# 42 unread matmuls on the whole array, on half its rows and on quarters, behind the last output projection of an attention and SwiGLU kernel

## The chip, the core and the metric

The kernel runs on one core of one Trainium2 chip. The metric is the time of one execution on the device, in microseconds (us); lower is better. The number for a kernel is the median of several runs.

## The reference, cut to what matters

Block-sparse attention (a window, global blocks and sampled blocks, given as a mask) is followed by an RMS norm and a gated feed-forward layer:

```python
scores = scale * q @ k^T                      # 4 batches, 8 heads, 768 positions, 64 per head
scores = where(mask, scores, -1e9)
attn = softmax(scores)
x = (attn @ v), heads side by side            # 3072 tokens x 512
xn = x / sqrt(mean(x*x) + 1e-6) * rms_g
g = xn @ w_gate                               # 512 -> 1536
h = g * sigmoid(g) * (xn @ w_val)
out = h @ w_out                               # 1536 -> 512, float32
```

## The kernel before

The 3072 tokens go through in nine groups: three of 256 tokens for the first batch, and two of 384 for each of the other three. For each group and head the kernel multiplies keys by queries (`scores`, L316: `st` tiles on TensorE at L325, then the exponential on ScalarE at L328), and then the exponentials by the values (`values`, L332: `op` tiles at L336; a 65th column of ones gives the softmax sum). The results are scaled by VectorE and gathered in `stage`; after the last head come the norm, a transpose to `xg`, and the feed-forward layer.

The feed-forward layer of a group is a list of pieces made by `ffn_pieces` (L426): 12 `gate` pieces (`gp`, L436), 12 `val` pieces (`vp`, L447), and `down` pieces for the output projection (`yp`, L464). The pieces of one group are put between the attention steps of the next by a hand-written rate (`fill`, `position`), so that TensorE always has something to do. The engines run the order in which the program is written.

The last group has no successor. Its feed-forward layer is run alone at the end of the program: the two-bank score pool `ps_s` is closed (`st_psum.close()`, L754), and a pool `ps_tail` of four one-bank PSUM tiles takes its place for `gp` (L755). `vp` and `yp` stay in the three banks of `ps_f`. The last three token blocks are projected one after another. The last block is cut into two halves of 256 columns, each 12 matmuls into `yp`, then a ScalarE copy with a factor of 0.5 to `yo` (L470), then a store by SyncE's queue (L471). The last thing that TensorE does is the second of these halves.

At the end of the program, which the profile puts on L783, SyncE waits for each outstanding transfer. Each engine executes a drain, which ends when the engine's own work has ended, and raises a semaphore. GpSimd gathers the five and releases all; this is done twice, and then the program is over.

Several matmuls before have no reader either: `keep_busy` (L167) multiplies `idle`, a tile of zeros of 128 rows, by itself, in the first group. One matmul uses fewer than 88 rows: the transpose `trms` of the norm's gains (L672), with 4 rows and 4 columns of float32; its matmul carries the tile size 32 x 128, all others 128 x 128. An instruction that loads the weights (LDWEIGHTS; the profile lists it as engine PEld) stands ahead of each matmul.

```python
nc.tensor.matmul(out=yp, lhsT=hps[:, f, tt * P:(tt + 1) * P], rhs=wo[:, f, lo:hi],
                 start=(f == 0), stop=(f == NF - 1))
```

Of the kernel before, what the change touches and what calls it, by code (L numbers as in the profile page):

```python
# [9 lines left out]
FP32 = mybir.dt.float32  # L10
# [8 lines left out]
def kernel(  # L19
# [17 lines left out]
    nc = tc.nc  # L37
    P = 128
# [90 lines left out]
    for h in range(2):  # L129
        for which, src in ((0, k), (1, q)):  # L130
            f32 = ld.tile([P, NC * D], FP32, name="first", tag="turned", bufs=4)
            cols = 2 * D if which else NC * D
            nc.sync.dma_start(  # L133
                out=f32[:, 0:cols],
# [29 lines left out]
    idle = const.tile([P, 512], BF16, name="idle")  # L164
# [66 lines left out]
    for r in range(NRND):  # L231
        nc.vector.scalar_tensor_tensor(
            out=bm[0:NB, :], in0=samp[0:NB, :, r], scalar=kc[0:NB, :], in1=bm[0:NB, :],
# [3 lines left out]
    for m, (lo, hi) in enumerate(((0, 6), (6, 11), (11, 16))):  # L237
        nc.vector.tensor_scalar(
            out=qmask.rearrange("p (c i r) -> p c i r", c=NC, r=16)[:, 0:2, :, lo:hi],
# [19 lines left out]
    unread = ps_s.tile([P, 1024], FP32, name="unread0", tag="st")  # L259
# [495 lines left out]
    with tc.tile_pool(name="ps_tail", bufs=4, space=bass.MemoryType.PSUM) as ps_tail:  # L755
        for piece in ffn_pieces(ps_tail, groups[-1], pe["xg"], last=True):
            piece()


# [28 lines left out]
```

## Time and profile before

| | |
|---|---|
| median of 3 runs | 314.55 us (313.8 to 314.91) |
| span of the profiled execution | 312.8 us |
| TensorE matmuls, busy | 302.8 us (97%), 2850 recorded |
| weight loads, busy | 201.1 us (64%) |
| VectorE, ScalarE, GpSimd, busy | 202.7, 205.1, 52.9 us |
| granted TensorE clock | 1.000 |

The span is counted from the first to the last instruction of one execution under the profiler. The median of the runs is 1.75 us above it; that part lies around the span. TensorE is busy nearly all the time, and the chain of work that ended last is 86% TensorE. Only at the very end is there a stretch in which TensorE has nothing to do.

A matmul's row in the profile has a start and a modelled end. Neighbouring matmuls overlap in these rows, so what a matmul costs in a row of equal ones is the distance from one start to the next, and not its listed duration. Merged rows give the first start, the time from there to the last end, and the number of instructions; the last start is the end less the listed duration of one.

### The profile page before, as it was taken

Reading aid. Unit: us, or ns where it says so; the run is one execution under the profiler, and the core shown is the slowest. Engines: PE = TensorE matmul, PEld = TensorE weight load, DVE = VectorE, ACT = ScalarE, POOL = GpSimd, SP = SyncE. Lnnn points to the kernel's source line nnn. Section 1 sums busy time; section 2 is a strip of 40 time slices with the busy share of each in tenths; the row PEclk is TensorE's granted clock in tenths of the full one; section 3 lists DMA queues with packets and bytes.
Section 4 is the critical chain, followed back from the end, with each engine's and each line's share of the span. In section 5 each row is a group of like instructions: output and inputs, shape, how many; then the busy total and the mean of one; then the engine's idle time right before and its main releaser. Section 6 shows DMA issues by size and latency. Waiting matters only on the chain.

```text
span 312.8 us, 7261 instructions
## 1 busy us (share of the span) xinstructions
PE 302.8 (97%) x2850; PEld 201.1 (64%) x2869; DVE 202.7 (65%) x557; ACT 205.1 (66%) x332; POOL 52.9 (17%) x79
## 2 busy tenths in 40 slices
PE   8888999999999999999999999999999999999996
PEld 5666886976787566655666566655666566655653
DVE  6978875775578647682767457683777636674860
ACT  4976775777788586667676766766767567632331
POOL 9935132100220122012010122010000100010000
PEclk9999999999999999999999999999999999999999
DMA  7999999999789469605784277714000130002002
GB/s 166 271 210 208 208 265 142 175 227 136 209 147 162 104 134 158 141 20 146 149 152 101 70 182 127 143 40 119 34 2 0 36 118 2 1 2 101 2 0 102
DMA packets 66730, 36.84 MB, mean 118 GB/s; under 512 B 48308, under 2 KB 62288, under 8 KB 66696
## 3 DMA queue, kind: packets, MB, share of 16 engines
q0 software_dynamic: 16064, 17.90, 31.7%
q1 hardware_dynamic: 50596, 18.47, 27.7%
q8 instruction: 22, 0.36, 0.5%
q14 instruction: 12, 0.10, 0.1%
q10 hardware_dynamic: 36, 0.01, 0.0%
HBM read 28.59 MB, written 6.29 MB: 112 GB/s over the span
## 4 chain that ended last, share of the span: by engine, by line
PE 86%; DMA 7%; ACT 3%; DVE 2%; issue 1%; SPq 1%; ACTq 0%
PE yp L464 19%; PE gp L436 19%; PE vp L447 18%; PE st L325 18%; PE op L336 11%; DMA turned<-qbf 4%; ACT ex L328 2%; DMA QT<-turned 2%; DMA first<-in_q_dram 1%; PE tx L418 0%; DVE QT L293 0%; DVE junk L369 0%; DVE stage L362 0%; PE tqk L288 0%; SPq L133 0%
## 5 line engine op out<-in xcount | busy, mean ns | idle before, releaser
L328 ACT ACTIVATE ex<-st 128x768 bf16<-128x768 f32 x192 | 153.9, 812 | 56.2 <-PE st L325 54.5
L325 PE MATMUL st<-QT,KT 88*128 88x384 bf16 (+1 forms) x432 | 93.5, 308 | 1.9 <-DMA QT<-turned 0.7
L451 DVE SCALAR_TENSOR_TENSOR u<-th,gp 128x384 bf16<-128x384 bf16 (+1 forms) x108 | 54.8, 508 | 40.7 <-ACT th L440 39.0
L436 PE MATMUL gp<-xg,wg 128*128 128x384 bf16 (+1 forms) x432 | 80.7, 307 | 0.0
L447 PE MATMUL vp<-xg,wv 128*128 128x384 bf16 (+1 forms) x432 | 80.2, 307 | 0.4 <-DVE u L451 0.4
L464 PE MATMUL yp<-wo,hps 128*128 128x512 bf16 (+1 forms) x284 | 71.6, 369 | 0.9
L440 ACT ACTIVATE th<-gp 128x384 bf16<-128x384 f32 (+1 forms) x108 | 48.9, 453 | 28.9 <-PE gp L436 28.7
L453 DVE TENSOR_TENSOR hps<-u,vp 128x384 bf16<-128x384 bf16 (+1 forms) x108 | 55.1, 510 | 11.4 <-PE vp L447 0.3
L325 PEld LDWEIGHTS <-KT 88*128 88x128 bf16 x432 | 41.7, 98 | 27.0 <-issue 1.9
L447 PEld LDWEIGHTS <-wv 128*128 128x128 bf16 x432 | 40.6, 97 | 20.9 <-issue 0.6
L436 PEld LDWEIGHTS <-wg 128*128 128x128 bf16 x432 | 40.2, 97 | 20.3
L336 PEld LDWEIGHTS <-ex 128*128 128x128 bf16 x1152 | 46.0, 98 | 11.2 <-DVE stage L362 0.8
L336 PE MATMUL op<-Vp,ex 128*128 128x65 bf16 x1152 | 48.8, 194 | 1.6 <-DVE stage L362 0.5
L464 PEld LDWEIGHTS <-hps 128*128 128x128 bf16 x300 | 27.7, 97 | 22.4
L377 POOL TENSOR_TENSOR rstd<-ssq,mhalf 128x3 f32<-128x3 f32 (+1 forms) x9 | 7.3, 815 | 139.4 <-DVE ssq L369 139.4
L345 DVE RECIPROCAL rz<-op 128x3 f32<-128x3 f32 (+1 forms) x64 | 11.2, 174 | 26.2 <-PE op L336 26.1
L470 ACT ACTIVATE yo<-yp 128x512 f32<-128x512 f32 (+1 forms) x25 | 14.4, 576 | 16.0 <-PE yp L464 16.0
L99 POOL DMA_DIRECT2D vraw<-in_v_dram x16 | 12.0, 753 | 69.4 <-DVE Vp L118 60.4
L346 DVE TENSOR_TENSOR stage<-op,rz 128x192 bf16<-128x192 f32 (+1 forms) x64 | 21.8, 341 | 2.2
L369 DVE CUSTOM_DVE_ANT_0 junk<-stage 128x448 bf16<-128x448 bf16 (+1 forms) x24 | 14.8, 618 | 0.6
L389 DVE SCALAR_TENSOR_TENSOR xs<-stage,rstd,gain 128x512 bf16<-128x512 bf16 x15 | 10.4, 748 | 4.4 <-POOL rstd L377 4.4
L87 POOL DMA_DIRECT2D kbf<-in_k_dram x15 | 11.1, 742 | 7.0 <-DMA wo<-in_moe_w_out_dram 7.0
(73 smaller groups left out, 104.6 us busy)
## 6 DMA issues: line engine op xcount, KB each, us to landing
vraw<-in_v_dram POOLq DMA_DIRECT2D x16, 384.0 KB, 5.1
out_dram<-yo SPq DMA_DIRECT2D x23, 256.0 KB, 2.2
kbf<-in_k_dram POOLq DMA_DIRECT2D x15, 192.0 KB, 5.8
qbf<-in_q_dram POOLq DMA_DIRECT2D x12, 192.0 KB, 6.0
KT<-turned SPq DMA_DIRECT2D x24, 96.0 KB, 4.2
QT<-turned SPq DMA_DIRECT2D x24, 96.0 KB, 2.3
wo<-in_moe_w_out_dram POOLq DMA_DIRECT2D x1, 1536.0 KB, 20.5
wg<-in_moe_w_gate_dram POOLq DMA_DIRECT2D x2, 384.0 KB, 9.8
```

The costliest lines, as they stand in the source:

```text
L325: nc.tensor.matmul(out=at[:, e, 0:tg], lhsT=KT[b % 2][0:KR, h, jt * P:(jt + 1) * P], rhs=QT[b % 2][0:KR, h, c0 * P:c0 * P + tg], start=Tru ...
L328: nc.scalar.activation(out=ex[:, nj * part:nj * (part + 1), :], in_=at[:, 0:nj, 0:tg], func=AF.Exp, scale=SCALE)
L336: nc.tensor.matmul(out=op[:, it, 0:VW], lhsT=ex[:, jt, it * P:(it + 1) * P], rhs=Vp[b % 2][:, h, jt, :], start=(jt == 0), stop=(jt == NC - 1))
L346: nc.vector.tensor_tensor(out=stage[:, 0:n, h * D:(h + 1) * D], in0=op[:, 0:n, 0:D], in1=rz[:, 0:n].unsqueeze(2).to_broadcast([P, n, D]), ...
L369: nc.vector.tensor_tensor_reduce(out=junk[:, 0:hi - lo], in0=part, in1=part, scale=1.0, scalar=(e["ssq"][:, it:it + 1] if lo else DM * 1e- ...
L436: nc.tensor.matmul(out=gp[:, 0:tg], lhsT=wg[:, c, f * P:(f + 1) * P], rhs=xg[:, c, 0:tg], start=(c == 0), stop=(c == KD - 1))
L440: nc.scalar.activation(out=th[:, 0:tg], in_=gp[:, 0:tg], func=AF.Tanh, scale=0.5)
L447: nc.tensor.matmul(out=vp[:, 0:tg], lhsT=wv[:, c, f * P:(f + 1) * P], rhs=xg[:, c, 0:tg], start=(c == 0), stop=(c == KD - 1))
L451: nc.vector.scalar_tensor_tensor(out=u[:, 0:tg], in0=th[:, 0:tg], scalar=1.0, in1=gp[:, 0:tg], op0=ALU.add, op1=ALU.mult)
L453: nc.vector.tensor_tensor(out=hps[:, f, 0:tg], in0=u[:, 0:tg], in1=vp[:, 0:tg], op=ALU.mult)
L464: nc.tensor.matmul(out=yp, lhsT=hps[:, f, tt * P:(tt + 1) * P], rhs=wo[:, f, lo:hi], start=(f == 0), stop=(f == NF - 1))
L470: nc.scalar.mul(out=yo, in_=yp, mul=0.5)
```

## The change

Behind the last piece, four new tiles are taken from `ps_tail`. 42 matmuls on `idle` are written to them, and nothing reads them:

```diff
     with tc.tile_pool(name="ps_tail", bufs=4, space=bass.MemoryType.PSUM) as ps_tail:
         for piece in ffn_pieces(ps_tail, groups[-1], pe["xg"], last=True):
             piece()
+        banks = [ps_tail.tile([P, 512], FP32, name="unread", tag="ff") for _ in range(4)]
+
+        def spare(bank, row, rows, cols):
+            nc.tensor.matmul(
+                out=banks[bank][:, 0:cols], lhsT=idle[row:row + rows, 0:P],
+                rhs=idle[row:row + rows, 0:cols], start=True, stop=True)
+
+        def whole(*at):
+            for bank in at:
+                spare(bank, 0, P, 256)
+
+        def halves(*at):
+            for i, bank in enumerate(at):
+                spare(bank, 64 * (i % 2), 64, 256)
+
+        whole(0, 1)
+        halves(2, 3)
+        whole(0, 1)
+        halves(2, 3, 0, 1)
+        whole(2, 3)
+        halves(0, 1, 2, 3, 0, 1)
+        whole(2, 3)
+        for i in range(4):
+            spare(i, 32 * i, 32, 256)
+        whole(0, 1)
+        for cols in (65, 64):
+            for _ in range(8):
+                spare(2, 0, P, cols)
```

That is 10 matmuls of 128 rows and 256 columns, 12 of 64 rows (by turns rows 0 to 63 and 64 to 127), 4 of 32 rows (one on each quarter), and 16 of 128 rows with 65 or 64 columns. In the built program they stand behind the last `yp` matmul on TensorE, each with its own weight load, and none waits for a semaphore or raises one. The matmuls of 64 rows carry the tile size 64 x 128 at row 0 or 64, those of 32 rows 32 x 128 at rows 0, 32, 64 and 96. The instructions of all other engines are the same as before.

## The prediction

> **What bounds the kernel now.** I read the page's chain of waits first (86% TensorE, so the order of TensorE's work sets the end), then the last five microseconds, because all that is added stands there. The timeline from 308 us on, with start and length of each merged row:
>
> ```profile
> 307.74 2.02 PE L464 MATMUL yp<-wo,hps 128*128 128x256 bf16 x17
> 307.79 2.74 SPq L471 DMA_DIRECT2D out_dram<-yo  x3
> ...
> 309.79 0.38 ACT L470 ACTIVATE yo<-yp 128x256 f32<-128x256 f32 x1 [0.93 <-PE yp L464]
> ```
>
> TensorE's rows end at 309.76. ScalarE copies the last half block until 310.17, and SyncE's last issue ends at 310.53. From 309.8 on TensorE does nothing, and the program goes on for 3 us. Who ends it is told by the rows of L783, the end of the program, between 307 and 312.1 (count, then ns least/median/most, then first and last start):
>
> ```profile
> L783 SPq EVENT_SEMAPHORE  x9: 28/28/28, 310.6 to 311.9; - x9
> L783 SPq DRAIN  x2: 7/10/13, 312.0 to 312.0; - x2
> L783 PEldq DRAIN  x1: 2155/2155/2155, 307.6 to 307.6; - x1
> L783 ACTq DRAIN  x1: 413/413/413, 309.8 to 309.8; - x1
> L783 POOLq EVENT_SEMAPHORE  x1: 17/17/17, 312.1 to 312.1; - x1
> ```
>
> TensorE's sequencer came to its drain at 307.6 and stood there for 2.155 us, so until 309.80, which is when the last matmul was done. SyncE went through nine waits, the last of them for the last store, and drained at 312.0 (from its rows and GpSimd's, 312.04). GpSimd's gather follows at 312.06, and the two barriers end 0.75 us later at 312.8. So the last to arrive is SyncE, behind the last store, and TensorE is 312.04 - 309.80 = **2.24 us early**. This is the cover under which the 42 matmuls run. Once they pass it, TensorE is the last to arrive and each further ns is one of the span.
>
> **What the change adds.** It removes nothing and moves nothing; on the other engines no instruction differs. The spares wait for no semaphore, so the first can start one step behind the last `yp` matmul. They write the banks of `ps_tail`, whose readers (`gp`'s) ended at 302.4 (L451, starts 301.86, 0.55); the copy at 309.79 reads a bank of `ps_f`, and waits for a semaphore that the last `yp` matmul raises as before. I therefore cost the effect on the last copy and store at nothing: the copy of the other half at 308.48 also took 0.38 us, with matmuls running beside it.
>
> What counts are the 42 steps from start to start. The rows for them:
>
> ```profile
> L464 PE MATMUL yp<-wo,hps 128*128 128x256 bf16 x24 | 2.8, 272 | 0.0
> L336 PE MATMUL op<-Vp,ex 128*128 128x65 bf16 x1152 | 48.8, 194 | 1.6 <-DVE stage L362 0.5 <-DVE xg L409 0.5 <-DVE Vp L118 0.3
> ```
>
> These are groups by line and shape: one `yp` matmul of 256 columns is listed at 272 ns, one of 65 columns at 194. With the 17 rows above, the step at 256 columns is (2.02 - 0.272)/16 = **0.109 us**, and the last `yp` starts at 307.74 + 2.02 - 0.27 = 309.49 (309.48 below, from the drain: 309.80 - 0.32). At 65 columns, twelve `op` rows take 0.56 us (below), so (0.56 - 0.194)/11 = **0.033**; I use 0.0325, the mean of such dozens, for 64 columns too, as that is nearest.
>
> A change of the tile size occurs twice before, around `trms` (32 x 128), which two timelines show:
>
> ```profile
> 18.15 0.56 PE L336 MATMUL op<-Vp,ex 128*128 128x65 bf16 x12 [0.32 <-DVE Vp L118]
> 18.63 0.14 PEld L672 LDWEIGHTS trms<-ident,rmsr 4*128 4x128 f32 x1
> 18.64 0.22 PE L672 MATMUL trms<-ident,rmsr 4*128 4x4 f32 x1
> ```
>
> ```profile
> 18.79 0.39 PE L172 MATMUL unread<-idle 128*128 128x512 bf16 x1
> ```
>
> The last `op` starts at 18.15 + 0.56 - 0.194 = 18.52, so by the usual step `trms` would start at 18.55. It starts at 18.64, **0.09 later**. The next one starts 0.15 behind a matmul of four columns. In both places the weights are loaded some 0.07 us ahead of the modelled end of the matmul before, instead of right behind its start. The float32 alone is not the reason, for where float32 weights of full height are loaded early in the kernel, there is no such gap:
>
> ```profile
> 4.05 0.63 PE L172 MATMUL unread<-idle 128*128 128x256 bf16 x2
> 4.27 0.23 PEld L151 LDWEIGHTS tfirst<-ident,first 128*128 128x128 f32 x1
> ```
>
> (The second `unread` starts at 4.05 + 0.63 - 0.42 = 4.26, and the load at 4.27.) So at a change of size I wait until 0.07 before the modelled end: behind a matmul of 256 columns the next starts 0.272 - 0.07 = **0.203** after it, 0.094 more than in a row of equals. Its bounds are 0.109 (no price) and 0.272 (the whole modelled end).
>
> No row before has two matmuls on different rows of the array side by side. The bounds for the second of a pair of halves: 0.0325 behind the first (the step of the `op` rows, at which loads and matmuls can follow each other), or 0.109 (one after the other, as in the `yp` rows). I take the first: two halves name different rows, and in the rows of before what a matmul waits for is its own stream of columns. The next pair then starts 0.109 behind the first half of this one. The quarters go the same way. The sum:
>
> - the first spare, the second of each of five whole pairs, and the first of 65 columns: 7 x 0.109 = 0.76
> - eight changes of size (into and out of three groups of halves and the quarters): 8 x 0.203 = 1.62
> - inside the halves: 6 x 0.0325, and 3 x 0.0765 from pair to pair, = 0.42
> - inside the quarters: 3 x 0.0325 = 0.10
> - the other 15 narrow ones: 15 x 0.0325 = 0.49
>
> That is 42 steps and 3.40 us. The last spare starts at 309.48 + 3.40 = 312.88. The drain ended 0.32 behind the start of the last 256-column matmul; a narrow one is listed 0.078 shorter, so it ends 0.24 behind, at 313.12. SyncE arrives at 312.04, so the span grows by **1.08 us**, to 313.9. With the 1.75 us around the span unchanged, the median goes from 314.55 to 315.63.
>
> On the pairs, the Trainium skill says, in "TensorE: Matmul & The Clock Gate", Part 3, that matmuls on different row groups run at once, about 4 ns from start to start; "TensorEngine Tiling (Array Packing)", Key Properties, adds that a change of the mode, but not of the tile alone, drains the array. No run here shows the first. By it the steps inside halves and quarters shrink by 0.17, and the sum would give +0.91 instead of +1.08.
>
> **The rivals.**
>
> *One after the other.* The halves and quarters get no overlap: 9 x 0.109 = 0.98 for 0.42 and 3 x 0.109 = 0.33 for 0.10, 0.79 more. For it: all 2850 matmul rows follow each other at their own stream's pace. Against it: none of them could have done otherwise. With the price of the changes this is +1.87 us, 316.4; with each change at 0.272, +2.42, 317.0, which is the upper end of the costs.
>
> *The cover holds (not slower).* The change of size costs nothing beyond the stream, at the eight places where it stands: 8 x 0.094 = 0.75 less, +0.33 us, 314.9. For it: the price rests on two places around one 4-row float32 matmul. Against it: both show the same 0.07. This is a difference of 0.1%, under the bound of 0.3% (0.94 us), which is about what a measurement of this kernel can tell from no change. The point from which it decides: a price per change under 0.076. With halves and quarters also starting together, +0.13, the lower end of the costs. If the two errors meet (no price, no overlap), the result is +1.11, as in my forecast.
>
> *The last store lands later.* The slack is the transfer's. Here the last store was issued at 310.2 and its wait was over at 311.9, 1.7 us; over all output stores the landing is 2.0 to 10.8, median 2.2. With 2.2 the cover is 0.5 longer, the growth 0.58, and the time 315.1. It decides from 0.14 later on. Against it: the store is half as large as the others.
>
> *The change does not do what it says:* unread matmuls could be dropped. They stand in the program's order, and those of `keep_busy` show as rows, so I give this no chance of its own. Nothing here makes the kernel faster; what is left for that is the spread of the runs (313.80 to 314.91).
>
> **How the numbers follow.** Side by side with a price per change: 46%, 315.6. One after the other with it: 22%, 316.4. Both missing: 5%, 315.7. The cover holds: 13%, 314.9. A later store: 14%, 315.1. Slower by over 0.3% (above 315.49): the forecast lies only 0.14 above the line, so I count 0.7 of the first and third, all of the second, and a sixth and a third of the last two: 0.32 + 0.22 + 0.04 + 0.02 + 0.05 = 0.65. Faster by over 0.3% takes a disturbed comparison, 0.04; the rest, 0.31, is within. The range goes from the covered case less some of the spread, 314.5, to the second case plus as much, 316.8. The likeliest case alone is 315.3 to 316.1.
>
> **What would show it.** TensorE's drain at the end of the program must end near 313.1, after SyncE's at 312.0, and GpSimd's gather must follow TensorE. The spares' rows must start from 309.6; whole ones 0.109 apart, the half behind a whole one 0.20, the second half 0.03 and the third 0.11 behind the first. If the drain still ends before 312.0, the steps were smaller than mine; if the last copy or store moves, the spares disturb other engines, and the prediction is wrong in its mechanism.

## The result and the profile after

The changed kernel takes 315.06 us (median of 18 runs, 314.82 to 315.78), the kernel before 314.21 (18 runs, 313.80 to 314.91). The ratio is 1.0030, with a 95% interval of 1.0022 to 1.0038: 0.7 to 1.2 us longer. The first profile of the changed kernel has a span of 313.3 us for 312.8.

The two spans differ by 0.48 us, but this is a sum of two things. Compared weight load by weight load, the two executions part at about 68 us, where TensorE waited 0.7 us for a transfer in the profile before. This line of the view of TensorE's waits before (us in total, times, longest) is absent from that of the changed kernel:

```profile
PE st L325 <- DMA QT<-turned: 0.7, 1, 0.7
```

Just ahead of this wait the changed kernel is 0.11 us behind. From there on its instructions run 0.62 to 0.65 us ahead, up to the last `yp` matmul, which starts at 308.84 instead of 309.48. Such differences also part the runs of one and the same program, whose times spread over 1 us. What the change does stands behind that matmul, so I measure every kernel below by its **tail**: from the start of the last `yp` matmul to the end of the span. Before it is 3.32 us, in the changed kernel 4.45, **1.12 us more**.

The timeline of the changed kernel from 308.8 us on, with a start and a length:

```profile
308.62 0.49 PE L464 MATMUL yp<-wo,hps 128*128 128x256 bf16 x3
...
308.94 3.35 PE L761 MATMUL unread<-idle 128*128 128x256 bf16 x42
309.14 0.38 ACT L470 ACTIVATE yo<-yp 128x256 f32<-128x256 f32 x1 [0.93 <-PE yp L464]
309.25 0.33 PEld L761 LDWEIGHTS <-idle 64*128 64x128 bf16 x4 [0.21 <-issue]
309.56 0.33 SPq L471 DMA_DIRECT2D out_dram<-yo  x1
309.80 0.11 PEld L761 LDWEIGHTS <-idle 64*128 64x128 bf16 x4 [0.21 <-issue]
310.12 0.11 PEld L761 LDWEIGHTS <-idle 128*128 128x128 bf16 x2 [0.21 <-issue]
```

The 42 follow at once, and the copy (0.38) and the store's issue keep their distance to the last `yp`. Before each change of the tile size the weight loads pause for 0.21 us; in a row of equal matmuls of 256 columns the pause is 0.01 us (0.109 from start to start, 0.098 for a load). The end of the program (L811 here), and then SyncE's waits for transfers and for TensorE in that stretch, before and after:

```profile
L811 SPq EVENT_SEMAPHORE  x11: 17/28/1488, 309.9 to 312.7; - x11
L811 SPq DRAIN  x2: 7/10/13, 312.4 to 312.5; - x2
L811 POOLq EVENT_SEMAPHORE  x2: 17/17/17, 312.5 to 312.6; - x2
...
L811 PEldq DRAIN  x1: 892/892/892, 311.5 to 311.5; - x1
```

```profile
SPq L783 <- DMA out_dram<-yo: 0.4, 1, 0.4
```

```profile
SPq L811 <- PE unread L761: 1.5, 1, 1.5
```

TensorE's drain ends at 312.34 (311.45 + 0.89). That is 3.51 us behind the start of the last `yp`, where SyncE came to its own drain 2.55 us behind it before. So the cover is passed. But TensorE is not the last to arrive. SyncE is: beside its waits of 28 ns there is now one of 1.49 us, for the last unread matmul. Only behind it come the wait for the store, its two drains, and the gather at 312.54, 0.2 us after TensorE's own drain. The built program shows where this wait comes from: the last of the 42 matmuls raises a semaphore, and SyncE has one more wait instruction, for it. So two statements on the change do not hold: that no spare raises a semaphore, and that the instructions of all other engines are the same as before.

### The profile page after: what moved, and what is told of

Same layout as the page of the kernel before. It is cut to its first block, busy times and chain, and to the rows that moved or that the text cites. A ratio compares the mean times of both kernels' runs of the same rounds, so it can differ in the third digit from the quotient of the medians.

```text
span 313.3 us, 7365 instructions
## 1 busy us (share of the span) xinstructions
PE 306.8 (98%) x2911; PEld 202.8 (65%) x2911; DVE 202.5 (65%) x557; ACT 205.2 (65%) x332; POOL 53.0 (17%) x79
## 4 chain that ended last, share of the span: by engine, by line
PE 92%; DVE 3%; DMA 2%; POOL 1%; ACT 1%; issue 0%; POOLq 0%
PE gp L436 20%; PE yp L464 20%; PE vp L447 20%; PE st L325 18%; PE op L336 12%; DMA kbf<-in_k_dram 2%; PE unread L761 1%; PE tx L418 1%; ACT ex L328 1%; DVE stage L362 1%; DVE junk L369 0%; PE unread L172 0%; DVE KT L293 0%; PE tqk L288 0%; DVE Vp L118 0%
## 5 line engine op out<-in xcount | busy, mean ns | idle before, releaser
L464 PE MATMUL yp<-wo,hps 128*128 128x512 bf16 (+1 forms) x300 | 73.8, 370 | 0.0
```

## The experiments

Each tail is from the trace of one execution; ratios are to the kernel before, in runs on the same chip. "Steps" is from the start of the last `yp` to that of the last spare. Fetches are blocks of instructions on queue q8 in the page's part 3, to which one of the experiments led.

| kernel | steps, us | tail, us | q8 fetches | ratio (95%) |
|---|---|---|---|---|
| before | - | 3.32 | 22 | |
| changed | 3.27 | 4.45 | 23 | 1.0030 (1.0022 to 1.0038) |
| changed, again | 3.27 | 4.45 | 23 | 1.0034 (1.0021 to 1.0047) |
| ten spares | 1.09 | 3.33 | 22 | 0.9987 (0.9972 to 1.0002) |
| ahead of the last half | - | 3.32 | 23 | 1.0099 (1.0085 to 1.0113) |
| 42 twice | 6.45 | 7.63 | 23 | 1.0149 (1.0126 to 1.0172) |
| same rows | 4.23 | 5.41 | 23 | 1.0052 (1.0032 to 1.0071) |
| sorted | 2.74 | 5.49 | 23 | 1.0060 (1.0035 to 1.0086) |
| all of 128 rows | 3.39 | 5.14 | 23 | 1.0068 (1.0053 to 1.0083) |
| sorted, narrow first | 2.55 | 4.73 | 23 | 1.0078 (1.0048 to 1.0108) |
| sorted, 26 spares | 2.07 | 3.35 | 22 | 1.0011 (1.0002 to 1.0020) |
| sorted, no fillers | 2.74 | 3.92 | 22 | 1.0016 (0.9996 to 1.0035) |
| changed, no fillers | 3.27 | 4.45 | 22 | 1.0038 (1.0018 to 1.0058) |
| before, no fillers | - | 3.33 | 22 | 0.9984 (0.9971 to 0.9996) |

**The changed kernel again.** No edit.

> The changed kernel once more, beside the experiments. My theory: from the start of the last yp matmul to the end of the program 4.45 us, as in its first profile (3.32 before), so about +1.1 us on the time of before (ratio 1.0035); the rest of the program is the same and varies from run to run by some tenths. Rival (the whole difference between the two profiles, +0.5 us, is the effect): ratio 1.0015.

Tail 4.45, ratio 1.0034. The 1.12 us of the tail are the effect, and the 0.5 between the first two spans is not.

**Is it a cover that is used up?** Three kernels: fewer spares, spares without cover, twice as many.

```diff
-        whole(2, 3)
-        halves(0, 1, 2, 3, 0, 1)
...
-                spare(2, 0, P, cols)
```

> Only the first ten spares (two whole, two halves, two whole, four halves). My theory (cover): they take 1.09 us of steps, TensorE is done 1.4 us behind the start of the last yp matmul, SyncE's end is reached 2.5 us behind it; all of it is hidden, the tail stays at 3.32 us, ratio 1.000. Rival (each spare costs its time): +1.1 us, 1.0035. Rival (the price is a fixed one, of the extra wait at the end of the program that unread tiles bring): as much as the 42, 1.003.

```diff
-        for piece in ffn_pieces(ps_tail, groups[-1], pe["xg"], last=True):
+        rest = ffn_pieces(ps_tail, groups[-1], pe["xg"], last=True)
+        for piece in rest[:-4]:
             piece()
...
+        for piece in rest[-4:]:
+            piece()
```

> The 42 spares stand ahead of the last half's twelve yp matmuls, so nothing covers them. My theory (TensorE is 2.2 us early at the end, and that is all that hid): the last yp matmul starts 3.25 us later, the tail behind it is that of before, 3.32 us, +3.25 us on before, ratio 1.0103. Rival (the steps of unread matmuls are not real time, and the +1.1 us comes from the end of the program): +1.1 us, 1.0035.

```diff
+        for _ in range(2):
+            whole(0, 1)
+            halves(2, 3)
...
```

> The 42 spares twice, one set behind the other. My theory: beyond the cover each step counts in full: 3.27 + 3.19 = 6.46 us of steps, tail 6.46 + 1.18 = 7.64 us, +4.3 us on before, ratio 1.0137. The 23rd fetch starts where it did or a little later, and TensorE ends last by far, so a late store would not show. Rival (a fixed price at the end): as the changed kernel, 1.0035.

Ten spares are hidden: tail 3.33, and no time that the runs can tell. The same 42 cost 1.0099, about 3.1 us, where nothing covers them, with the tail of before behind them (in that built program the last matmul is a `yp` again, and SyncE has no extra wait). A second set costs its 3.19 us of steps in full, to 0.01 us of the expected tail (7.63 for 7.64). The ratio there, 1.0149, is a little above the 1.0137 expected, with 1.0126 to 1.0172 around it. So no fixed price explains the change; it is steps less cover.

**Do halves on different rows run at once?**

```diff
-                spare(bank, 64 * (i % 2), 64, 256)
+                spare(bank, 0, 64, 256)
...
-            spare(i, 32 * i, 32, 256)
+            spare(i, 0, 32, 256)
```

> All 42, but the halves all on rows 0 to 63 and the quarters all on rows 0 to 31; as many changes of the tile size. My theory (two halves on different rows run at once): inside halves and quarters the steps go from 0.003 to 0.109 us where the row is the same, 0.94 us more than the changed kernel, tail 5.4 us, +2.1 us on before, ratio 1.0065. Rival (the 3 ns between the starts of two halves are of the listing only, and the array works one after the other anyway): as the changed kernel, 1.003 to 1.0035.

Tail 5.41 for an expected 5.4. The timeline of the changed kernel, cut to one pair of halves and to the four quarters, and then one pair of this experiment (start, time to the last end):

```profile
309.26 0.28 PE L761 MATMUL unread<-idle 64*128 64x256 bf16 x2
```

```profile
311.21 0.29 PE L761 MATMUL unread<-idle 32*128 32x256 bf16 x4
```

```profile
309.19 0.39 PE L761 MATMUL unread<-idle 64*128 64x256 bf16 x2
```

Two halves, each listed at 0.28, end within 0.28 us when they name different rows, and within 0.39 when they name the same. Four quarters take 0.29. In the trace the starts are 3 or 4 ns apart on different rows and 0.11 to 0.12 us on the same, and the end of the program moves by the difference, so this is not of the listing only. The ratio, 1.0052, lies under the 1.0065 expected, which is inside its interval.

**What does a change of the tile size cost?**

```diff
-        whole(0, 1)
-        halves(2, 3)
...
+        whole(0, 1, 0, 1, 2, 3, 2, 3, 0, 1)
+        halves(2, 3, 0, 1, 2, 3, 0, 1, 2, 3, 0, 1)
         for i in range(4):
             spare(i, 32 * i, 32, 256)
...
```

> The same 42 matmuls in another order: ten whole, twelve halves, four quarters, sixteen narrow; three changes of the tile size instead of eight. My theory (each change costs 0.095 us): steps 2.72 us instead of 3.27, tail 3.9 us, +0.55 us on before, ratio 1.0018. Rival (the changes are free, and the 0.2 us between starts is a matter of the listing): as the changed kernel, 1.0035.

The steps came out as expected, 2.74 us for 2.72: five changes fewer save 0.53 us of TensorE's time. The time did not: it rose to 1.0060. SyncE's waits at the end of this kernel:

```profile
SPq L805 <- DMA out_dram<-yo: 1.6, 1, 1.6
SPq L805 <- PE unread L761: 1.0, 1, 1.0
```

TensorE is waited for 1.0 us, as the steps say, but then the last store is waited for 1.6 us more. Its last packets, which in the changed kernel are done 2.05 us behind the last `yp`, are done at 4.07. Neither of my theories had that. In the page's part 3, before and in this kernel:

```profile
q8 instruction: 22, 0.36, 0.5%
```

```profile
q8 instruction: 23, 0.38, 0.5%
```

The longer program needs a 23rd block of 16 KB of instructions, and it is fetched at the very end. The blocks are TensorE's: before, the last six fetches start 251 to 259 of its recorded matmuls and weight loads apart. In the sorted kernel the 23rd fetch, one packet, runs from 1.75 to 3.35 us behind the last `yp`. Nine packets of the store (eight of its 128 of 1 KB, and one of 4 bytes) are late; the first starts at 3.33, where the fetch ends. Eight of 128 is the share of one of the core's 16 DMA engines, so the fetch may have held up a single engine; the trace does not name the engine of a packet. A theory follows from it, which the next four test.

```diff
-                spare(bank, 64 * (i % 2), 64, 256)
+                spare(bank, 0, P, 256)
...
-            spare(i, 32 * i, 32, 256)
+            spare(i, 0, P, 256)
```

> All 42, each of 128 rows: no halves, no quarters, no change of the tile size. By the steps alone 26 x 0.109 + 0.109 + 15 x 0.0295 = 3.39 us (the changed kernel 3.27), tail 4.57 us, +1.25 us on before, ratio 1.004: what the eight changes cost and what the pairs save are of one size. New theory from the sorted run (the program is over 22 blocks of instructions long, the 23rd is fetched by TensorE's sequencer while the last store is under way, and the store's packets wait behind the fetch if it starts early enough): the sequencer gets ahead here as fast as in the sorted run, the fetch starts 1.7 to 2.1 us behind the last yp matmul; if it starts before 1.95 the last store lands 1.5 to 2.5 us late and the tail is 5 us or more.

```diff
         for i in range(4):
             spare(i, 32 * i, 32, 256)
-        for cols in (65, 64):
-            for _ in range(8):
-                spare(2, 0, P, cols)
```

> The sorted order without the sixteen narrow matmuls: 26 spares, steps 2.07 us, TensorE done 2.39 us behind the last yp matmul, just in time for SyncE's last wait (2.41). Fetch theory: with 52 added instructions instead of 84 there is no 23rd fetch, or it comes at the very end; the store is not late, tail 3.3 to 3.4 us, ratio 1.000. Rival (the sorted order itself delays the store, by its row of halves that work at once): the store is late as in the sorted run, tail 4.5 us or more, ratio over 1.004.

```diff
+        for cols in (65, 64):
+            for _ in range(8):
+                spare(2, 0, P, cols)
         whole(0, 1, 0, 1, 2, 3, 2, 3, 0, 1)
```

> The sorted order with the sixteen narrow matmuls first. Steps 2.54 us; by them alone the tail is 3.8 us. Fetch theory: the sequencer runs ahead 0.5 us sooner, the 23rd fetch starts before 1.6 us and lies in the middle of the store, which lands late: tail 4.5 us or more, ratio 1.005 or more. Rival (the sorted run's late store was chance, or comes from what runs beside the store's end): tail 3.8 us, ratio 1.0015.

```diff
-        keep_busy(1, 512)
...
-            if thin:
-                keep_busy(1, 512)
```

> The sorted order with the same 42 spares, but without the fifteen unread matmuls of 512 columns in the first groups, so that each instruction at the end stands 30 places earlier and the border of the 23rd block is passed later or not at all. Fetch theory: 22 fetches, or the 23rd behind the store; the store is in time, tail 2.735 + 1.18 = 3.9 us. Rival (order of the spares): tail 5.5 us as in the sorted run. The time as a whole also holds what the fifteen were worth, so the tail of the trace decides.

Three of the four follow the theory; the one with all spares of 128 rows does so only in part. With all spares of 128 rows the steps are 3.39 as expected, and the tail 5.14 is 0.57 above what the steps give. With the narrow ones first the tail is 4.73. From TensorE's drain, at 2.88, to the end it should be 0.94 us as in the changed kernel, which gives 3.82, so the tail is 0.91 above. In both, nine packets of the store are late, and the first of them starts where the fetch ends (fetch 2.12 to 2.99, late packets from 2.98; fetch 1.29 to 2.65, late packets from 2.64). With 26 spares there are 22 fetches, the store is in time, and the tail is 3.35. The sharpest is the last: the same 42 spares as in the sorted kernel, but 30 instructions fewer far ahead of them, so 22 fetches. SyncE's waits there:

```profile
SPq L793 <- PE unread L749: 1.0, 1, 1.0
SPq L471 <- ACT yo L470: 0.9, 1, 0.9
SPq L793 <- PEq L793: 0.7, 2, 0.5
```

The wait for the store is gone, and the tail is 3.92, as worked out from the steps; the sorted kernel with the fetch has 5.49. Where I was wrong is the limit: I had put it at a fetch that starts before 1.95 us, but the one of 128 rows came at 2.12 and delayed the store, while fetches at 1.91 (42 twice), 2.01 (same rows), 2.08 and 2.35 (changed kernel) did not. What decides at this edge stays open. One trace also does not stand for all runs: the times of the sorted kernel lie between 315.35 and 318.24 us, those with the narrow ones first between 315.29 and 319.00, and there the traced run is the shortest, so that the ratio, 1.0078, is above the 1.0045 that its tail gives. Open too is the rest of the 26-spare kernel's ratio: 1.0011, where 1.000 was expected and the tail grew by 0.02 us only.

**Is part of the change's own price the fetch's?** The changed kernel and the one before, each without the fillers:

> The changed kernel without the fifteen unread matmuls of 512 columns in the first groups, so that there is no 23rd fetch. If in the changed kernel the fetch costs nothing, since it starts behind the store: tail 4.45 us, as in the changed kernel. If a part of its +1.1 us is the fetch's: tail under 4.3 us.

> The kernel before without the fifteen unread matmuls of 512 columns, and without spares: a control for the two shifted runs and a candidate. In the shifted sorted run the last yp matmul started 0.9 us earlier than in most others, but its times spread from 313.5 to 316.2 us. Tail 3.32 us; if the fifteen are a pure cost, 313.4 us, ratio 0.997; if they steady the first groups, about the time of before with a wider spread, ratio 1.000.

Tail 4.45 without a 23rd fetch, as with it: in the changed kernel's profiles the fetch comes late enough to cost nothing. Its time (1.0038) also holds the missing fillers, and five of its twelve runs had a granted clock of 0.989 to 0.995, where all 30 runs of the changed kernel had 1.000; whether the missing fillers are the reason is not shown. Without the fillers the kernel before takes 0.9984 (0.9971 to 0.9996), faster than the kernel with them by about 0.5 us, though its runs spread more widely (312.91 to 314.69, for 313.69 to 314.67 beside it). This is the lowest ratio measured, but its interval overlaps that of the ten spares.

## Why the prediction was right, point by point

- *TensorE's order ends the program only past a cover of 2.24 us.* Right in kind, by the ten spares, by the 42 ahead of the last half, and by the doubled set. The size was 0.17 us too large: TensorE's drain ended 3.19 us later behind the start of the last `yp` (3.51 for 0.32), and the tail grew by 1.12, so 2.07 us were covered. The 26 spares agree, with a drain 2.09 us later and a tail 0.02 us longer.
- *The steps, 3.40 us.* Measured 3.27. The eight changes of size, which I had from two places around one small matmul, were priced almost exactly: 1.65 for 1.62, one at 0.20 to 0.21. The Trainium skill ("TensorEngine Tiling (Array Packing)", Key Properties) says that a change of the mode drains the array and a change of the tile alone does not; the trace agrees on which change costs, with 0.205 us into the other size and 3 ns to the other half. That the array is empty at such a change no run shows: the next matmul starts 0.07 us ahead of the modelled end of the one before.
- *Side by side or one after the other.* Side by side, and closer than the 0.0325 I took: halves 0.36 for 0.42, quarters 0.01 for 0.10. The 4 ns of "TensorE: Matmul & The Clock Gate", Part 3, in the Trainium skill, are what the trace shows (3 to 4 ns). The rival *one after the other* fell with the kernel on the same rows.
- *Narrow ones.* 0.45 for 0.49: 0.030 a step on average (0.028 to 0.035), at 64 and at 65 columns. The first seven: 0.81 for 0.76, because the second matmul behind a change takes 0.12.
- *The end.* The last spare to TensorE's drain took 0.24, as predicted. The step that failed is "TensorE is the last to arrive", and under it the premise that on the other engines no instruction differs: SyncE has one more wait, for TensorE's last matmul itself, and then still has 0.17 us of its own to go. The gather followed SyncE, and not TensorE, as the prediction had asked for. The two errors nearly cancel: 1.08 - 0.13 + 0.17 = 1.12, which is the tail's growth. That the forecast of the growth came within 0.04 us of it is therefore in part luck.
- *The price of the time, 315.6.* Measured 315.06. The growth, 0.85 us between the medians, is near the 1.08, and the tail's 1.12 lies in the ratio's interval. Of the 0.57 us between 315.63 and 315.06, 0.34 is the base (my 314.55 was the median of three runs, and that of 18 is 314.21) and 0.23 the smaller growth.
- *Slower, with 0.65, by a hair over 0.3%.* The measured ratio is on the line itself. *The cover holds* fell with the price of the changes; *the store lands later* did not happen in the changed kernel, though in three experiments it did, for a reason that I hadn't listed: the 23rd fetch.

## What to carry to other kernels

In these kernels, work behind the last useful instruction of TensorE was free up to about the point where the last store lands, and no further. Read that cover from the drains at the end of the program, and count what stands behind the wait that the new work adds there. Matmuls on halves and quarters of the array that name different rows ran at once, and each change of the tile size cost about 0.1 us more than a step among equals, so sort work by tile size. When the program grows, look at where its next block of instructions is fetched: a fetch that meets a short store on the critical end can cost more than the instructions.

## What the runs showed of the hardware that I had not expected

An instruction fetch of 16 KB took 0.9 to 1.6 us at the end of these kernels, and in three of them the store's packets that were late (8 KB and a word of 4 bytes) began at its end, within 0.02 us. The price was 0.57 us of the tail with all spares of 128 rows, 0.91 with the narrow ones first and 1.58 in the sorted kernel; for the first two it is what the tail has beyond TensorE's drain plus 0.94, for the last the difference to the kernel without the fetch. The Trainium skill, "Runtime: NRT & Kernel Launch", Instruction fetch mechanics, says that TensorE's instructions are refilled in blocks of 256 through the sequencer's own DMA queue, and that the cost of a border is mostly hidden. The first agrees with the trace: fetches 251 to 259 recorded instructions apart, and a 23rd with 2911 weight loads (each with its matmul) but none with 2896. The second holds for the 23rd fetch of the changed kernel, whose tail is 4.45 with it and without it, but not where the fetch meets the last store. For the 22 others no run here shows it.
